# W1's loads of the merged stage: a pause while block 2's tokens are turned, then even distances

## The chip, the cores and the metric

The kernel runs on one core of one Trainium2 chip. A time is the device time of one execution in microseconds (us). Timed runs give a median; a separate profiled execution gives the trace, whose span (first to last instruction) is a little shorter than that execution's time.

## The reference

Three layers follow each other. All tensors are float32.

```python
# attention with random features: q, k, v are (4, 8, 576, 64)
q_p, k_p = phi(q_s), phi(k_s)            # exp(x @ omega.T - |x|^2/2 - max)
num = q_p @ (k_p.T @ v); den = q_p @ k_p.sum(0)
x = (num / den) as 2304 tokens of 512
# gated MLP, 512 -> 1536 -> 512
x = (sigmoid(x @ w_gate) * (x @ w_val)) @ w_out
# soft mixture of 8 experts with 4 slots each
logits = x @ phi                          # 2304 x 32
slots  = softmax(logits, over tokens).T @ x     # 32 x 512
slot_out[e] = relu(slots[e] @ w1[e]) @ w2[e]    # w1[e] 512 x 1024, w2[e] 1024 x 512
out = softmax(logits, over slots) @ slot_out
```

The change touches the loads of `w1` and four loads of `w2`. W1 is 16.8 MB, and the chip's on-core memory has no room for it while the MLP runs, so its pieces are loaded as buffers of the MLP come free.

## The kernel before, in words

The 2304 tokens are handled as five blocks: four of 512 (numbers 0 to 3) and one of 256 (number 4). Every float32 product of the MLP is three matmuls: each operand is split into a rounded high part and a remainder (`hi_of` on ScalarE, ACT, or VectorE, DVE; `lo_of` on GpSimd, POOL, or DVE). The MLP's weights lie in a DRAM buffer `wscr`, from where they are loaded again for each block or pair of blocks into `ws`.

The stages are, in order: attention and the first blocks (0 to 340 us), the pair of blocks 2 and 3 (to about 505 us), the merged stage (about 505 to 600 us), and the expert layers with the output.

**The merged stage** (`tail_jobs`, L1561) runs the last part of block 3, the products with `w_out` (`down_b`), together with the whole MLP of block 4 (`up_passes`, `down_c`). It has twelve steps, one for each 128 columns of the hidden layer. A step needs three weight pieces of 256 KB. `split_t` (L849) reads a piece from one of four slots of `ws`, splits it into a tile `w0`, `w1`, `w2` or `more`, and then `load_part` (L783) issues the load of a later piece into the same slot. These loads, `ws<-wscr`, are issued on SyncE's queue (SP). SP issues in order.

**Beside it** runs block 2's part in the expert layer (`m2_jobs`, L1650, with `moe2_chunks`, L1143): the logits, the turning of the block's tokens and the product into slots. The turning is four transposes on DVE (`chunk_x2`, L1108) and then sixteen moves of 64 KB between two buffers on the chip, `x2T<-x` (`chunk_back`, L1117), issued on SP too.

**W1's loads** (`load_w1`, L1163) are issued on ACT's queue, 512 KB each. The first eight (experts 0 and 1) have no floor, and the last two are issued late, when the slots are done. The other 22, and four loads of W2 into block 2's buffers (`free_x2`, L1198, on SP), take numbers 0 to 25 from one counter (`ring_of`, L1176) in the order in which the jobs are written: numbers 0 to 15 are experts 2 to 5, 16 is the first piece of expert 6, 17 and 18 two pieces of expert 7, 19 the next of expert 6, 20 to 23 the W2 loads, 24 and 25 the last of expert 6. A load with number k has the floor `BEGIN + PACE1 * k`, that is 478.0, 480.9, and so on to 550.5.

**What sets the order.** The kernel's text makes a list of operations with keys. A planner (`Plan.schedule`, L257) simulates them with a cost for each and hands out each engine's work in the order of the simulated times: an operation starts when its inputs and its buffer are ready, its engine is free and its floor (`plan.floor`) is past. Then the instructions are written down engine by engine in that order. A floor is a time of the plan, not of the chip: on the chip nothing waits for a clock. An engine issues its DMAs in the place that the plan gave them, each when its buffer is free. DMAs signal their end through eight counters, used in turn over both queues in the order of the plan, so a DMA is issued only when the one eight places before it has landed.

Of the kernel before, what the change touches and what calls it, by code (L numbers as in the profile page):

```python
# [81 lines left out]
M2 = 45.0  # L82
W1S = [1.0, 8.0, 15.0, 22.0, 24.0, 36.0, 50.0, 63.0, 29.0]
W2S = 2.0
BEGIN = 478.0
PACE1 = 2.9
TAIL0, TAIL1 = 2.75, 4.2
READY = 12.0
EARLY = 30
# [351 lines left out]
def body(ctx, tc, nc, qkT, tok, von, omT, wall, phi, w1, w2, ident_d, srep_d, rrep_d, mask_d, out):  # L441
    plan = Plan(nc)
# [713 lines left out]
    def pieces(tag, bufs=1, n=4):  # L1156
        if tag == "g1":
            halves = [half_region(k, F32) for k in range(2)]
            return [halves[c // 2][:, 1024 * (c % 2):1024 * (c % 2) + 1024] for c in range(n)]
        t = T([128, 1024 * n], tag, F32, bufs)  # L1160
        return [t[:, 1024 * c:1024 * c + 1024] for c in range(n)]

    def load_w1(x=None, cs=range(4)):  # L1163

        if x is None:
            e = len(W1)
            x = pieces(EXTAGS[e], 3 if EXTAGS[e] == "XT" else 1)
            W1.append(x)
        e = next(k for k, y in enumerate(W1) if y is x)
        for c in cs:  # L1170
            if 2 <= e < E - 1 or e == E - 1 and c > 1:
                plan.floor = BEGIN + PACE1 * ring_of("w1")
            ACT.dma_start(out=x[c], in_=w1[e, :, 1024 * c:1024 * c + 1024])
        plan.floor = 0.0

    def ring_of(name):  # L1176
        ring[name] = ring.get(name, -1) + 1
        return ring[name]

    def load_w2():  # L1180

        while len(W2) < len(ORDER2) and free:
            e, c = ORDER2[len(W2)]
            W2[e, c] = free.pop(0)
            SP.dma_start(out=W2[e, c], in_=w2[e, c])
# [12 lines left out]
    def free_x2():  # L1198

        for x in pieces("x2", 1, 2) + pieces("x2T", 1, 2):  # L1200
            free.append(x)
            plan.floor = BEGIN + PACE1 * ring_of("w1")
            load_w2()
        plan.floor = 0.0

# [42 lines left out]
    def last_slots():  # L1248
# [50 lines left out]
        si = T([128, 4, NSLOT], "si")  # L1299
        DVE.tensor_copy(out=si, in_=ps)  # L1300
        load_w1(W1[E - 1], (0, 1))
        plan.t = t0 + 7.0
        pr = bank("o3")[:, 0:NSLOT]
# [354 lines left out]
    for g, (j, f0, f1) in enumerate(GROUPS):  # L1658
        span = SPAN[g]
        if j == NB - 1:  # L1660
            m2_jobs(0, start + 3.0, 60.0)
            jobs += [(start + 4.0, "ex", load_w1), (start + 12.0, "ex", load_w1)]
            start = pair_jobs(start)
            jobs += [(start + W1S[k], "ex", load_w1) for k in range(4)]
            jobs += [(start + W1S[4 + c], "ex", lambda c=c: load_w1(W1[6], (c,))) for c in range(4)]
            jobs.append((start + W1S[4] - 0.01, "ex", big_regions))
            jobs.append((start + W1S[8], "ex", lambda: load_w1(W1[7], (2, 3))))
            jobs.append((start + M2 + W2S, "ex", free_x2))
            m2_jobs(PAIR[0], start + 1.0, M2)
            start = tail_jobs(start)  # L1670
            continue
        for f in range(f0, f1):
            jobs += moe_jobs(i, start + span * (f - f0) / (f1 - f0), span / (f1 - f0))
            i += 1
        units, a0, a1 = {0: (range(4, 8), LATE0 + 5 * LATE1, start + 0.92 * span),
                         1: (range(8, 16), start + LATE8 * span, start + span + SPAN[2] - READY - EARLY)}.get(g, ((), 0, 0))
        att = [c for u in units for c in step_chunks(u)]
        jobs += [(a0 + (a1 - a0) * k / len(att), "att", c) for k, c in enumerate(att)]
        if g == 2:
            m2_jobs(1, start + span / (f1 - f0), span * 0.7)  # L1680
        start += span
# [78 lines left out]
def build(nc, arrays):  # L1760
    args = [nc.dram_tensor(n, a.shape, mybir.dt.from_np(a.dtype), kind="ExternalInput").ap()
            for n, a in arrays.items()]
    args.append(nc.dram_tensor("out_0", (NTOK, DM), F32, kind="ExternalOutput").ap())
    with tile.TileContext(nc, schedule_with_timeline_sim=True) as tc:
        with ExitStack() as ctx:
            body(ctx, tc, nc, *args)
# [8 lines left out]
```

## Time and profile before

| | us |
|---|---|
| median of 3 runs (lowest, highest) | 665.77 (665.5, 667.17) |
| the profiled execution | 664.72 |
| its span | 662.6 |
| TensorE matmul (PE) busy | 640.8 (97%) |
| VectorE (DVE) busy | 482.3 (73%) |
| ScalarE (ACT) busy | 408.7 (62%) |
| GpSimd (POOL) busy | 266.4 (40%) |
| mean granted TensorE clock | 0.994 of full |

PE is busy nearly throughout, with float32 matmuls in three passes. The profile's page says that the DMA engines moved 134.27 MB, 203 GB/s in the mean, and shares out the chain of work that ended last as PE 85%, DVE 5%, DMA 4%. All engine work carries the line of one helper (L434), so rows are told apart by tile names: `ga`, `va`, `o` and `fl` are banks of accumulators, `w`, `more` split weights, `ws` the slots for weights, `g` and `XT` regions into which W1 is loaded, `x2T<-x` the turning moves.

### The profile page before, as it was taken

Reading aid. Unit: us, or ns where it says so; the run is one execution under the profiler, and the core shown is the slowest. Engines: PE = TensorE matmul, PEld = TensorE weight load, DVE = VectorE, ACT = ScalarE, POOL = GpSimd, SP = SyncE. Lnnn points to the kernel's source line nnn. Section 1 sums busy time; section 2 is a strip of 40 time slices with the busy share of each in tenths; the row PEclk is TensorE's granted clock in tenths of the full one; section 3 lists DMA queues with packets and bytes.
Section 4 is the critical chain, followed back from the end, with each engine's and each line's share of the span. In section 5 each row is a group of like instructions: output and inputs, shape, how many; then the busy total and the mean of one; then the engine's idle time right before and its main releaser. Section 6 shows DMA issues by size and latency. Waiting matters only on the chain.

```text
span 662.6 us, 12685 instructions
## 1 busy us (share of the span) xinstructions
PE 640.8 (97%) x4236; PEld 510.3 (77%) x4236; DVE 482.3 (73%) x1460; ACT 408.7 (62%) x937; POOL 266.4 (40%) x255
## 2 busy tenths in 40 slices
PE   7998999999999999999999999999999979999995
PEld 6675777778888788777877888788888878988663
DVE  5989998999899877788788966646647735545323
ACT  5999888889988867878775653443543412234012
POOL 1544444355544433336335455455553333321100
PEclk9999999999999999999999999999999989999998
DMA  7888666878886656533527732131226879736988
GB/s 251 314 274 265 240 216 207 259 234 275 277 279 222 208 152 231 187 96 112 160 80 240 224 108 62 36 95 36 79 77 223 242 247 313 269 106 226 405 337 242
DMA packets 61440, 134.27 MB, mean 203 GB/s; under 512 B 6848, under 2 KB 20928, under 8 KB 61376
## 3 DMA queue, kind: packets, MB, share of 16 engines
q1 hardware_dynamic: 55552, 116.11, 53.7%
q10 hardware_dynamic: 5824, 17.37, 8.0%
q8 instruction: 33, 0.54, 0.3%
q14 instruction: 31, 0.25, 0.1%
HBM read 113.00 MB, written 17.30 MB: 197 GB/s over the span
## 4 chain that ended last, share of the span: by engine, by line
PE 85%; DVE 5%; DMA 4%; issue 2%; SPq 1%; ACT 1%; POOL 1%; DVEq 0%; ACTq 0%; POOLq 0%
PE o L434 27%; PE fl L434 23%; PE va L434 18%; PE ga L434 17%; DVE g L434 2%; SPq L434 1%; DMA x2T<-x 1%; DMA ws<-wscr 1%; DMA g<-in_von 1%; DVE ga_a L434 1%; DMA g<-qscr 1%; DMA qscr<-g 1%; DVE g1b L434 0%; DVE x2T L434 0%; DVE x L434 0%
## 5 line engine op out<-in xcount | busy, mean ns | idle before, releaser
L434 POOL TENSOR_TENSOR w<-ws,w 128x512 fp32r<-128x512 f32 (+1 forms) x96 | 112.5, 1172 | 178.6 <-ACT w L434 46.8
L434 PE MATMUL o<-gt,w 128*128 128x512 f32 (+1 forms) x396 | 103.7, 396 | 0.0
L434 ACT ACTIVATE g<-g 128x128 f32<-128x128 f32 (+5 forms) x214 | 78.2, 422 | 15.5 <-DVE g L434 10.5
L434 PE MATMUL ga<-XT,w 128*128 128x512 f32 (+1 forms) x312 | 84.7, 400 | 2.3 <-POOL XT L434 1.3
L434 PE MATMUL fl<-g,g 64*128 64x128 f32 (+4 forms) x686 | 83.3, 313 | 3.6 <-DVE g L434 1.7
L434 PEld LDWEIGHTS o<-gt,w 128*128 128x128 f32 x396 | 71.7, 189 | 19.3 <-issue 3.3
L434 ACT ACTIVATE w<-ws 128x512 fp32r<-128x512 f32 (+1 forms) x87 | 49.4, 569 | 58.1 <-PE o L434 29.4
L434 PEld LDWEIGHTS fl<-g,g 64*128 64x128 f32 (+2 forms) x686 | 60.2, 182 | 24.2 <-issue 9.6
L434 PE MATMUL va<-XT,w 128*128 128x512 f32 x288 | 78.5, 403 | 0.0
L434 PEld LDWEIGHTS ga<-XT,w 128*128 128x128 f32 x312 | 54.9, 188 | 16.8 <-POOL XT L434 2.1
L434 PEld LDWEIGHTS va<-XT,w 128*128 128x128 f32 x288 | 52.5, 188 | 11.7 <-issue 1.3
L434 ACT ACTIVATE x2T<-g 128x512 f32<-128x512 f32 x72 | 46.0, 668 | 4.4 <-DVE x L434 3.5
L434 ACT ACTIVATE g1b<-g1b,g 128x128 f32<-128x128 f32 x128 | 40.5, 390 | 1.2 <-DVE g L434 1.2
L434 PE MATMUL o<-XT,w 128*128 128x256 f32 x264 | 36.8, 290 | 4.0 <-DVE ws L434 4.0
L434 PEld LDWEIGHTS o<-XT,w 128*128 128x128 f32 x264 | 35.2, 197 | 5.8 <-DVE ws L434 4.5
L434 DVE TENSOR_SCALAR x2T<-x2T 128x512 f32<-128x512 f32 (+1 forms) x72 | 36.3, 515 | 1.2 <-ACT x2T L434 1.0
L434 DVE CUSTOM_DVE_ANT_0 g<-fl,g 128x128 f32<-128x128 f32 x142 | 32.2, 284 | 3.1 <-PE fl L434 2.9
L434 POOL TENSOR_TENSOR g<-g 128x512 f32<-128x512 f32 (+1 forms) x20 | 23.0, 1149 | 28.5 <-DMA g<-in_tok 10.4
L434 ACT ACTIVATE ga_a<-ga_a 128x512 f32<-128x512 f32 x48 | 30.0, 624 | 3.2 <-DVE ga_a L434 2.9
L434 POOL TENSOR_TENSOR w<-x,w 128x512 fp32r<-128x512 f32 x17 | 21.8, 1285 | 23.6 <-ACT w L434 8.8
L434 DVE SCALAR_TENSOR_TENSOR x2T<-g,x2T 128x512 int32<-128x512 int32 x36 | 28.2, 785 | 0.1
L434 DVE TENSOR_REDUCE g<-g 128x8 f32<-128x512 f32 (+3 forms) x33 | 23.9, 726 | 5.9 <-POOL g L434 2.9
(310 smaller groups left out, 1361.7 us busy)
## 6 DMA issues: line engine op xcount, KB each, us to landing
ws<-wscr SPq DMA_DIRECT2D x37, 512.0 KB, 3.9
g<-in_wall SPq DMA_DIRECT2D x36, 512.0 KB, 5.0
ws<-wscr SPq DMA_DIRECT2D x52, 256.0 KB, 4.2
wscr<-x SPq DMA_DIRECT2D x36, 256.0 KB, 4.6
g<-in_qkT SPq DMA_DIRECT2D x15, 576.0 KB, 5.0
g<-in_tok SPq DMA_DIRECT2D x15, 576.0 KB, 5.2
g<-in_w ACTq DMA_DIRECT2D x16, 512.0 KB, 4.3
XT<-in_w ACTq DMA_DIRECT2D x12, 512.0 KB, 4.9
```

The lines of the kernel that those rows point to most:

```text
L434: ins = getattr(self.eng[e], method)(*a, **k)
```

## The change

The 26 numbered loads get other floors. Numbers 0 to 3 go to 476.0, 478.5, 481.0 and 483.5. Number 4 goes to 476 + 28 = 504.0 (it was 489.6), and from there each number follows the one before at 2.5 (it was 2.9), so that number 25 has 556.5 (it was 550.5). Nothing else is edited; the planner orders all operations anew with these floors.

```diff
-BEGIN = 478.0
-PACE1 = 2.9
+BEGIN = 476
+PACE1, FIRST1, GAP1 = 2.5, 4, 28.0
...
             if 2 <= e < E - 1 or e == E - 1 and c > 1:
-                plan.floor = BEGIN + PACE1 * ring_of("w1")
+                plan.floor = BEGIN + w1_at(ring_of("w1"))
             ACT.dma_start(out=x[c], in_=w1[e, :, 1024 * c:1024 * c + 1024])
         plan.floor = 0.0
+
+    def w1_at(k):
+        return PACE1 * k if k < FIRST1 else GAP1 + PACE1 * (k - FIRST1)
...
         for x in pieces("x2", 1, 2) + pieces("x2T", 1, 2):
             free.append(x)
-            plan.floor = BEGIN + PACE1 * ring_of("w1")
+            plan.floor = BEGIN + w1_at(ring_of("w1"))
             load_w2()
```

## Rows read from the trace of the kernel before

**Rows 1.** Windows: us; busy of PE, PEld, DVE, ACT, POOL; clock, DMA share, GB/s.

```profile
520.00:530.00 10.00, 9.92 (x67) 8.74 (x66) 7.93 (x22) 3.97 (x7) 2.87 (x2) 1.00 0.91 257
530.00:540.00 10.00, 5.98 (x39) 5.41 (x38) 3.61 (x7) 1.02 (x2) 2.56 (x2) 0.92 0.93 313
...
560.00:570.00 10.00, 10.00 (x72) 8.49 (x71) 6.34 (x12) 1.68 (x4) 3.24 (x3) 1.00 0.83 297
...
590.00:600.00 10.00, 10.00 (x93) 7.21 (x91) 4.58 (x17) 6.01 (x15) 2.22 (x3) 1.00 0.16 52
...
620.00:630.00 10.00, 10.00 (x177) 5.62 (x173) 3.48 (x13) 0.00 (x0) 0.00 (x0) 1.00 1.02 413
```

**Rows 2.** Timeline of PE (start, duration, operation; in brackets idle time and releaser).

```profile
525.69 0.30 PEld L434 LDWEIGHTS ga<-ga_a,more 128*128 128x128 f32 x2 [0.28 <-ACT more L434]
...
533.69 0.63 PE L434 MATMUL va<-gt,more 128*128 128x512 f32 x2
538.34 2.93 PE L434 MATMUL o<-XT,w 128*128 128x256 f32 x12 [4.02 <-DVE ws L434]
```

**Rows 3.** Windows cut at PE's stop.

```profile
534.40:538.34 3.94, 0.00 (x1) 0.00 (x1) 0.78 (x3) 0.00 (x0) 0.31 (x1) 1.00 1.02 378
538.34:541.80 3.46, 3.46 (x16) 3.46 (x17) 1.54 (x2) 0.36 (x1) 0.96 (x1) 0.51 0.51 179
```

**Rows 4.** Chain of waits, 513 to 539 us: start, duration, what.

```profile
517.77 6.77 DMA x2T<-x
...
524.55 0.34 ACTq L434
...
530.91 1.07 POOL w L434
531.98 5.45 DMA ws<-wscr
...
537.52 0.43 DVE w L434
537.95 0.34 DVE ws L434
```

**Rows 5.** Timeline of ACT and POOL: the split `more`.

```profile
525.01 0.63 ACT L434 ACTIVATE more<-ws 128x512 fp32r<-128x512 f32 x1 [0.97 <-POOL w L434]
525.72 1.57 POOL L434 TENSOR_TENSOR more<-ws,more 128x512 fp32r<-128x512 f32 x1 [0.85 <-ACT more L434]
```

**Rows 6.** Timeline of SP's queue: the first and last moves, one between, the next load.

```profile
514.48 0.52 SPq L434 DMA_DIRECT2D x2T<-x  x1
...
524.20 0.51 SPq L434 DMA_DIRECT2D x2T<-x  x1
...
529.52 0.51 SPq L434 DMA_DIRECT2D x2T<-x  x1
530.12 0.53 SPq L434 DMA_DIRECT2D ws<-wscr  x1
```

**Rows 7.** Waits of SP's queue, 513 to 531 us: total, times, longest.

```profile
SPq L434 <- DMA g<-in_w: 3.5, 2, 2.8
```

**Rows 8.** DMA issues: KB, median us to landing; 513 to 530, then 300 to 500 us.

```profile
x2T<-x SPq DMA_DIRECT2D x16, 64.0 KB, 4.9
...
x2T<-x SPq DMA_DIRECT2D x32, 64.0 KB, 2.5
```

**Rows 9.** Timeline of ACT's queue: W1 issues with numbers 0, 11, 16 and 25.

```profile
498.79 0.33 ACTq L434 DMA_DIRECT2D g<-in_w  x1
...
531.75 0.34 ACTq L434 DMA_DIRECT2D g<-in_w  x1
...
551.75 0.33 ACTq L434 DMA_DIRECT2D g<-in_w  x1
...
578.28 0.34 ACTq L434 DMA_DIRECT2D g<-in_w  x1
```

**Rows 10.** Loads into `ws`, 548 to 590 us: issue to landing.

```profile
DMA to landing us min/median/max: 2.5/4.2/5.3
```

## The prediction

> **What bounds the kernel now.** I read the windows of ten microseconds first. TensorE (PE) is busy through nearly every one of them; the reader is to see the one that is not, 530 to 540 us, where PE has 5.98 of 10 us and the DMA engines a share of 0.93 [rows 1]. So time is to be had only where PE stops, and around the change it stops once. The timeline of PE shows the stop: the last matmuls before it end at 533.69 + 0.63 = 534.32, and the next twelve start at 538.34 after 4.02 us, released by VectorE (DVE) writing `ws` [rows 2]. Cut at that point, the windows show a second cost: over 538.34 to 541.80 the granted clock is 0.51, that is 1.2 in place of 2.4 GHz, while it is 1.00 in the idle piece before and 0.92 over the whole ten [rows 1, 3]. In those 3.46 us PE does what takes about half of that at full clock, so 3.46 / 2 = 1.73 us are lost. The stop costs 4.02 + 1.73 = 5.75 us.
>
> Why it stops I read from the chain of waits, backwards. PE waited for the DVE write of `ws` at 537.95, which stood in DVE's queue behind the cast `w` at 537.52, and that cast waited for a load of weights, `ws<-wscr`, issued at 531.98 and 5.45 us under way [rows 4]. The chain puts the issue at 531.98 down to GpSimd's (POOL's) `w`. I don't follow it there. The five weight slots are given back in the order of their splits, and the slot of this load was given back by the split before that one, `more` at 525.72 + 1.57 = 527.29 [rows 5]. The load was late because its queue was: SyncE (SP) issues in order, and before this load it had to issue sixteen moves `x2T<-x`, the turning of block 2's tokens, from 514.48 to 529.52, and one weight load at 530.12 [rows 6]. In program order the DMAs take eight completion counters in turn, over both queues, and each waits for the one eight places before it. That is why a move, which touches nothing that W1 touches, was issued only at 524.20: SP had stood for a W1 load, 2.8 us at the longest and 3.5 us in two waits [rows 6, 7]. The same tie runs the other way. The W1 issue on ScalarE's (ACT's) queue at 524.55 waited for a move that was 6.77 us under way [rows 4], and the split `more` queued behind it, with ACT idle for 0.97 us, then kept PE's weight load waiting for 0.28 us [rows 5, 2].
>
> The moves themselves are slow in this stretch: 4.9 us in the median from issue to landing, where the thirty-two moves of blocks 0 and 1, with only W1's eight loads without floor in that stretch, took 2.5 us [rows 8].
>
> **The change part by part.** No transfer is added or removed: 26 floored transfers (22 of W1, and 4 of W2 which share the counter) keep their sizes and queues, and only their earliest planned times move.
>
> First, when they run. A floor is a planned time, and the trace runs behind it by a shift that the W1 issues themselves show: 498.79 for floor 478.0 (number 0) is 20.8; 531.75 for 509.9 (number 11) is 21.9; 551.75 for 524.4 (number 16) is 27.4; 578.28 for 550.5 (number 25) is 27.8 [rows 9]. The step from 21.9 to 27.4 is the stop again, 5.5 us of shift that PE does not make up later. With the new floors and 21.7 us of shift, numbers 0 to 3 (476 to 483.5) run at about 497 to 505 us, and number 4 (504) at about 525.7. Between 505 and 525.7 no W1 load is issued, where there are seven now (numbers 3 to 9). The moves, which start at 514.48, lie in the pause.
>
> Then SP. Sixteen moves and two weight loads follow each other at the 0.6 us that a move's issue takes, 18 x 0.63 = 11.3 us, if no counter holds them up. A counter comes round after eight issues, 5 us; a landing of 2.5 us, as in blocks 0 and 1, is well inside, and even 4.9 us just is. So SP is through with the moves at about 525.8 in place of 530.0. ACT has no W1 issue to stand at: `more` starts about 0.8 us earlier, and its POOL half ends near 526.4. The late load is then issued at 526.4 instead of 531.98.
>
> What it needs: PE ran out of work at 534.32, and from landing (537.43) to PE's restart (538.34) passed 0.91 us, so a landing by 533.4 costs PE nothing. At 5.45 us, as now, it lands at 531.9; at 4.2 us, the median of the later weight loads with W1 beside them [rows 10], at 530.6. Even the slowest of 548 to 590 us, 5.3 us, leaves over a microsecond. I take 5.45, the row nearest in place. The slowest move of the turning, a smaller transfer, took 6.77 us; taken for the weight load it gives 533.2, still in time by 0.2 us. So the stop goes: 4.02 + 1.73 + the 0.28 of ACT's hold-up = 6.03 us. At the upper end the 0.97 us of ACT's idle time come back whole, 6.7 us; at the lower, a landing a microsecond later than any here leaves a short stop, 5 us.
>
> What is late next: the even train after the pause. It has 22 transfers in 504 to 556.5, 52.5 us, where they had 60.9 us. 524 KB per 2.5 us is 210 GB/s in place of 181; three weight loads of 262 KB per step of 7.05 us add 112. That is 321 GB/s against 292. The window 560 to 570 moved 297 GB/s at a share of 0.83 with PE busy for all of it, so 321 would be a share of 0.90; the same engines moved 413 GB/s at 620 to 630 [rows 1]. I price the faster train at nothing. Its cover is the time between a weight load's issue and its split, in which landings of up to 5.3 us cost PE no wait [rows 10]; without that cover each of seven further steps would pay. Below nothing it can't be: with fewer loads in flight no row here shows PE faster.
>
> The Trainium skill (DMA: Bandwidth & Descriptors, section "Where 436 GB/s comes from") says that HBM binds a core at some 358 GB/s. By it, 321 GB/s would have 37 GB/s left and the crowding rival below would be near; its time of 663 us would be mine. The trace disagrees: 413 GB/s out of HBM in [rows 1]. I go by the trace.
>
> Two smaller edits cost nothing. The first four loads come about 2 us earlier, beside PE work that needs few transfers. The last one, floor 556.5, runs at 556.5 + 22 = 578.5 where it ran at 578.28, and is followed by a stretch whose DMA share is 0.16 (590 to 600) [rows 1]. With the merged stage ending 6 us sooner it still lands before the expert layers, which come after 605.
>
> The sum is made against the profiled execution: 664.72 - 6.03 = 658.7 us. The runs shown have their median 1.05 us above it, 665.77, so the time that a median would show is 659.7 us.
>
> **The rivals.**
> *The resumed train crowds the weights once.* The weight loads of 525 to 534 us share the engines with four W1 loads instead of the moves. For it: at a share of 0.93 the late load needed 5.45 us, and landings spread. Against: the moves, which made the share high at only 257 GB/s (520 to 530), are done by then. If a stop of 1.5 us remains and the clock falls after it as it does now, the gain is 6.03 - 1.5 - 1.73 = 2.8 us: 663 us.
>
> *The W1 loads were not the cause.* The moves have short rows and one slow issuer; if they alone make SP late, the stop stays and the time is 665.8 us. Against: blocks 0 and 1, and SP's waits for W1 by name [rows 8, 7]. The case in which the pause lies beside the moves in time, so that the change does not do what it says, has the same price; it needs a shift wrong by 8 us or more, where the issues agree within 1.1 us before the stop.
>
> *Slower.* The place is the seven steps from 542 to 590 us. Each weight load there has so far landed in 5.3 us or less. If the train drives the engines to their limit, landings grow as they did around 524 to 532 us, to some 7 us, and every step waits 7 - 5.3 = 1.7 us: 7 x 1.7 = 11.9, with the clock falling at least once, 13.6, less 6.0 of gain: 7.6 us slower, 673 us. It decides from the point at which 321 GB/s can't be moved at a share under 1. Against it stands 413 GB/s in [rows 1].
>
> **How the numbers follow.** Forecast 0.74, one crowded stop 0.11, no gain 0.07, slower 0.08. A change of 0.3% is 2.0 us, about what a measurement of this kernel can tell from none. Faster by more: 0.74 + 0.11 = 0.85; within: 0.07; slower: 0.08. The forecast's own range is 658.5 to 661 us (6.7 to 5 us of gain, with the spread of the medians). Widened to take in the crowded stop, it is 658 to 664 us; the other two cases, with 0.15, and a little of the rest stay outside.
>
> **What would show it.** Right: no PE wait over 1 us between 525 and 600 us, granted clock 1.00 there, SP's list of waits without W1 loads up to 526, moves landing in about 2.5 us, last move issued before 526.5, and the whole chain after 540 shifted by 5.5 to 6.5 us. Wrong: a PE wait on `ws` again near 534, or new waits of DVE or ACT on `ws<-wscr` every 7 us after 540.

## The result, and the profile after

| | before | changed |
|---|---|---|
| median of 7 runs each, us | 667.17 | 662.54 |
| lowest and highest | 665.5, 668.73 | 660.38, 663.57 |
| ratio, 95% interval | | 0.9917 (0.9894 to 0.9940) |
| profiled execution, span | 664.72, 662.6 | 660.38, 658.6 |

The change made the kernel faster by 4.6 us in the medians; 6.0 had been forecast. The ratio's interval, taken of 667.17 us, is 4.0 to 7.1 us, so it holds both numbers. In a second comparison on the chip (run e10 below) the ratio was 0.9927 (0.9901 to 0.9953).

The windows of the changed kernel, with the columns of [rows 1]:

```profile
510.00:520.00 10.00, 10.00 (x84) 8.52 (x83) 6.91 (x13) 5.72 (x9) 2.77 (x3) 1.00 0.33 87
520.00:530.00 10.00, 10.00 (x71) 9.27 (x70) 6.59 (x16) 6.26 (x9) 3.89 (x3) 1.00 0.62 167
530.00:540.00 10.00, 9.15 (x64) 8.17 (x64) 7.17 (x13) 2.63 (x4) 4.98 (x4) 1.00 0.96 345
...
560.00:570.00 10.00, 10.00 (x68) 9.20 (x67) 4.27 (x8) 1.63 (x4) 3.88 (x3) 1.00 0.88 295
...
590.00:600.00 10.00, 10.00 (x91) 8.66 (x88) 6.82 (x28) 5.42 (x16) 2.59 (x2) 1.00 0.27 68
```

The reader sees the pause (a DMA share of 0.33 at 510 to 520, where it was 0.76), the resumed train (0.96 at 530 to 540) and what is left of the stop: PE is busy for 9.15 of those ten microseconds, where it was 5.98, and the clock is 1.00, where it was 0.92 [rows 1].

PE's one stop in the stage, in its timeline, and the wait of SP's queue on W1 in 513 to 531 us (total, times, longest), which answers to [rows 7]:

```profile
536.59 0.61 PE L434 MATMUL o<-XT,w 128*128 128x256 f32 x3 [0.85 <-DVE ws L434]
```
```profile
SPq L434 <- DMA g<-in_w: 1.8, 1, 1.8
```

That wait lies behind the late weight load in SP's queue: it ended at 530.29, when the W1 load issued at 525.82 had landed. No move and neither of the first two weight loads behind the moves stood for W1.

The DMA issues of 513 to 530 us (count, KB, median us to landing), against [rows 8]: the moves are twice as fast. Of the weight loads, the two in the pause are faster too (2.9 and 3.8 us, where their like took 5.3 and 4.9); the three issued from 527.00 on, beside the resumed W1 loads, take 6.2 to 6.5 us.

```profile
ws<-wscr SPq DMA_DIRECT2D x5, 256.0 KB, 6.2
x2T<-x SPq DMA_DIRECT2D x16, 64.0 KB, 2.6
```

The chain of waits that ended in this stop (start, duration, what), against [rows 4]:

```profile
527.42 0.20 DVE ws L434
527.63 6.38 DMA ws<-wscr
534.00 0.03 issue
...
534.13 0.43 DVE w L434
534.56 0.20 DVE cT L434
534.75 1.45 DVE ga_a L434
536.20 0.34 DVE ws L434
536.54 0.04 issue
```

The late weight load is issued at 527.63 instead of 531.98, but takes 6.38 us instead of 5.45, and between its landing and PE's restart lie two more operations of DVE, `cT` and `ga_a`.

**A measure with less noise.** The runs of one kernel spread over several microseconds, and most of that arises before the change has any effect: over the twelve profiles of the table the merged stage begins anywhere from 501.0 to 505.8 us. So I compare profiles by the time from the first of PE's twelve `o<-gt,w` (502.74 us before, 503.81 changed) to the end of the span: "the stage" from here on. Each kernel has one profile. The two of the changed kernel (changed and e10) differ by 0.65 us, as much as their stops do (0.85 and 1.51), so a difference of a few tenths between two kernels is not told by this measure.

```
kernel                     ratio (95%)             stage us  PE stop us  clock after it  moves land
before                     1                       159.90    4.02        0.51            4.9
changed                    0.9917 (0.9894-0.9940)  154.78    0.85        1.00            2.6
e10 changed, again         0.9927 (0.9901-0.9953)  155.43    1.51        1.00            2.3
e1  pause, old distance    0.9947 (0.9920-0.9973)  157.70    2.08        0.64            2.9
e2  distance, no pause     0.9953 (0.9927-0.9979)  158.71    3.07        0.58            4.6
e4  new order, old loads   0.9975 (0.9947-1.0002)  158.76    3.12        0.56            4.7
e3  old order, new loads   0.9898 (0.9869-0.9927)  154.30    none                        2.4
e8  old order, pause only  0.9892 (0.9857-0.9927)  154.44    none                        2.2
e9  old order, pace only   1.0013 (0.9985-1.0041)  161.74    3.74, 0.76  0.50            5.6
e7  old order, own counter 0.9900 (0.9863-0.9937)  155.21    0.82        1.00            4.9
e5  old order, few bytes   0.9928 (0.9904-0.9952)  155.42    1.19        1.00            2.4
e11 new order, later       0.9896 (0.9865-0.9926)  153.56    none                        2.1
```

Ratio: runs of the kernel against runs of before on the same chip; all other columns come from one profile each. "Moves land" is the median in the window from 510 or 513 to 530 us (532 in e2, 534 in e9, to take in all sixteen).

### The profile page after: what moved, and what is told of

The parts are those of the page before. It is cut to its first block, busy times and chain, and to the rows that moved or that the text cites. A ratio compares the mean times of both kernels' runs of the same rounds, so it can differ in the third digit from the quotient of the medians.

```text
span 658.6 us, 12689 instructions
## 1 busy us (share of the span) xinstructions
PE 639.2 (97%) x4236; PEld 508.8 (77%) x4236; DVE 484.6 (74%) x1460; ACT 410.5 (62%) x937; POOL 269.1 (41%) x257
## 4 chain that ended last, share of the span: by engine, by line
PE 76%; DMA 8%; DVE 7%; ACT 3%; issue 3%; SPq 1%; POOL 1%; DVEq 0%; POOLq 0%; ACTq 0%
PE o L434 24%; PE fl L434 20%; PE va L434 16%; PE ga L434 16%; DVE g L434 3%; DMA qscr<-g 2%; DMA g<-in_tok 2%; DMA ws<-wscr 2%; SPq L434 1%; DMA g<-qscr 1%; DMA g<-in_wall 1%; DVE ga_a L434 1%; ACT ga_a L434 1%; ACT g L434 1%; DVE g1b L434 1%
```

## The experiments

My theory: with the pause the moves, and the weight loads behind them on SP, are free of W1's loads, and that is the whole gain. The rivals: the closer distance makes it; or the planner, which got other floors, wrote another order for all engines, and that order makes it. The orders do differ: e3's expectation counts 168 of PE's matmuls and 56 of DVE's instructions in other places than before (the traces, which leave out buffer numbers, show 93 and 56), and some splits changed their engine.

**e1: the pause alone, at the old distance.**

```diff
-BEGIN = 476
-PACE1, FIRST1, GAP1 = 2.5, 4, 28.0
+BEGIN = 478.0
+PACE1, FIRST1, GAP1 = 2.9, 4, 26.0
```

> The old start and distance (478.0, 2.9) with the pause alone: number 4 at 504.0, the last at 564.9. Theory (the pause frees the moves, and the weight load behind them, from W1's loads): PE's stop near 536 us is under 1.5 us, the clock stays at 1.00, ratio to before 0.990 to 0.994. Rival (the closer distance makes the gain): the stop of some 4 us stays, ratio 0.998 to 1.002. The distance of 2.9 crowds the resumed loads less, so by the theory the stop is no longer than the 0.85 us of the changed kernel.

The moves were freed (2.9 us), but a stop of 2.08 us stayed and the time missed the theory's range. **e2: the distance alone.**

```diff
-PACE1, FIRST1, GAP1 = 2.5, 4, 28.0
+PACE1, FIRST1, GAP1 = 2.5, 26, 0.0
```

> The new start and distance (476, 2.5) without the pause: number 25 at 538.5, so that nine loads in place of seven fall between 505 and 525 us. Theory of the pause: the moves land in 4.9 us or more again, a stop of 4 us or longer stays near 536 us with the clock falling after it, ratio 0.999 to 1.006. Rival (the distance makes the gain): ratio 0.990 to 0.994.

The moves were slow and a stop of 3.07 us stayed, in kind as the theory expected, though shorter than its 4 us; yet the runs were faster than before by 0.5%, which was not expected. Both misses have one cause, as e8 and e9 below show: each set of floors gets another order from the planner, so neither run changed one thing. The next two hold the order.

**e3: the order of before, only the loads moved.** After the planner has run with the old floors, loads 4 to 25 alone are put elsewhere in its list; every instruction of PE, DVE, POOL and ACT other than the loads stays in its place.

```diff
-        for _, i, (e, method, a, k) in self.schedule():
+        order = list(self.schedule())
...
+        order.sort(key=lambda x: place_of(*x))   # load k >= 4: at TO(k), once its buffer is free
+        for _, i, (e, method, a, k) in order:
...
+def TO(k):
+    return 504.0 + 2.5 * (k - 4)
```

> The order of before for every engine's work, with only the numbered loads 4 to 25 moved to the places of the new floors (504 and then every 2.5); numbers 0 to 3 stay. Theory (transfers): the stop goes to under 1 us as the profile of before foretold it, ratio 0.989 to 0.993. Rival (the planner, given other floors, put 168 of PE's matmuls and 56 of DVE's operations in other places, and that made the gain): the stop stays at 3 to 4 us, ratio 0.998 to 1.002.

**e4: the order of the changed kernel, the loads put back** in the same way, with `TO(k) = 478.0 + 2.9 * k`.

> The order of the changed kernel for every engine's work, with the numbered loads 4 to 25 moved back to the places of the old floors (478.0 + 2.9 k). Theory (transfers): the moves land in about 5 us again and a stop of 3 us or more comes back, ratio to before 0.998 to 1.003. Rival (the planner's order): the stop stays under 1.5 us, ratio 0.990 to 0.994.

Together they answer. Moving the loads alone takes 5.60 us off the stage and leaves PE no stop at all. The new order alone takes off 1.14 us and leaves a stop of 3.12 us; its ratio, just under the theory's 0.998, can't be told from 1. The windows of e3 from 520 us on, where [rows 1] has 5.98:

```profile
520.00:530.00 10.00, 10.00 (x73) 9.18 (x72) 7.76 (x20) 3.21 (x6) 3.64 (x3) 1.00 0.69 213
530.00:540.00 10.00, 10.00 (x72) 9.12 (x72) 6.44 (x12) 2.35 (x5) 4.10 (x4) 1.00 0.96 339
540.00:550.00 10.00, 10.00 (x69) 9.21 (x69) 5.04 (x9) 2.91 (x5) 3.88 (x3) 1.00 0.98 348
```

PE never stops, although the share is 0.96 and more. With the loads at these places, the order that the planner wrote for the changed kernel therefore cost 0.5 to 1.1 us of stage (154.78 and 155.43 against 154.30). The ratios of runs don't settle this small difference; their intervals overlap.

**e8 and e9: pause and distance apart, in the old order.** As e3, with `TO(k) = 504.0 + 2.9 * (k - 4)` and `TO(k) = 476.0 + 2.5 * k`.

> The order of before for all work, loads 4 to 25 moved to 504 and then every 2.9 (the last at 564.9): the pause at the old distance, without the planner's new order. Theory (the pause frees the moves; the planner's order spoiled part of it with the pause at the old distance): no stop over 0.5 us, stage from the first twelve o<-gt,w to the end 154.0 to 154.8 us, ratio 0.988 to 0.992. Rival (the distance of 2.5 is needed for the gain): the stop of 2 us stays as with the pause alone in the planner's order, stage 157 us or more, ratio 0.994 to 0.997.

> The order of before for all work, loads 4 to 25 at 476 + 2.5 k (486 to 538.5): the new distance without the pause and without the planner's new order. Theory of the pause: moves land in 4.5 us or more, a stop of 4 us or longer near 538 us with the clock falling, stage 159.5 to 162 us, ratio 0.999 to 1.006. Rival (the distance makes the gain): stage under 156 us, ratio 0.989 to 0.993.

Both came as the theory said, but for e9's stop: 3.74 us, and an earlier one of 0.76, where one of 4 us or longer was expected. The pause takes off 5.46 us by itself, and the distance adds nothing to it that these profiles can tell (154.44 against 154.30). Without the pause the closer distance costs 1.84 us of stage in the one profile; the interval of its ratio has 1 in it. In e9 PE's stop and the clock behind it (windows with the columns of [rows 3]), and SP's waits for W1, are the picture of before, only worse:

```profile
541.41 2.93 PE L457 MATMUL o<-XT,w 128*128 128x256 f32 x12 [3.74 <-DVE ws L457]
```
```profile
541.41:545.00 3.59, 3.59 (x17) 3.59 (x17) 1.54 (x2) 0.48 (x1) 0.97 (x1) 0.50 1.01 383
```
```profile
SPq L457 <- DMA g<-in_w: 5.0, 4, 2.3
```

**e7: the bytes stay, the counters go.** What of W1's loads does the harm: their bytes in flight, or the eight counters which they share with SP's DMAs? Loads 4 to 9 go to another queue, which has counters of its own.

```diff
+            if 489.0 < self.floors[i] < 505.0:
+                e = "POOL"
             for e, method, a, k in [p[0] for p in k["parts"]] if method == "together" else [(e, method, a, k)]:
                 ins = getattr(self.eng[e], method)(*a, **k)
```

In the kernel the line that unpacks follows with the changed engine.

> The kernel before with the loads 4 to 9 issued on GpSimd's queue in place of ScalarE's, at the same planned times. Their transfers then run beside the moves as before, but take completion counters of their own, so that neither SP nor ScalarE can stand at a counter for them. If the counters carry the harm, SP's waits name no W1 load, the last move is issued before 527 us and PE's stop near 538 us falls under 1.5 us; ratio to before 0.990 to 0.995. If the bytes in flight carry it, the moves still land in 4.5 us or more, SP stands at the counters of its own moves, and a stop of 2.5 us or more stays; ratio 0.997 to 1.005. GpSimd's own time for issuing may add up to 6 us of its queue, which would show as later splits on GpSimd.

Its DMA issues of 510 to 530 us and SP's waits on DMAs:

```profile
g<-in_w POOLq DMA_DIRECT2D x5, 512.0 KB, 4.9
ws<-wscr SPq DMA_DIRECT2D x4, 256.0 KB, 4.8
x2T<-x SPq DMA_DIRECT2D x16, 64.0 KB, 4.9
```
```profile
SPq L436 <- DMA x2T<-x: 1.6, 2, 1.4
SPq L436 <- DMA ws<-wscr: 0.6, 1, 0.6
```

The moves are as slow as before (4.9 us), and still most of the gain is there: no wait of SP for W1, sixteen moves issued in 11.6 us (517.51 to 529.06) instead of 15.0, and the old stop gone. PE's one stop, 0.82 us, is another: it ends 2.6 us later in the stage (543.95 - 505.75 = 38.2 us from its start, against 35.6), and the load behind it, issued at 535.80 and 7.2 us under way, is the third after the one that was late before. The six issues took GpSimd 3.5 us in all. The last move came after the 527 us that I had named, but this stage began 3.0 us later than that of before. So the harm went mainly by the queues being tied to each other. The run takes two ties at once, SP's to W1's counters and ACT's to the moves'; it doesn't part them.

**e5: the counters stay, the bytes go.** As e3, but loads 4 to 9 keep their old places with 32 of 1024 columns, and the rest follows at the new places.

```diff
+        late = [(place_of(*x), x[1], (*x[2][:3], {n: y[:, 32:1024] for n, y in x[2][3].items()}))
+                for x in order if 489.0 < self.floors[x[1]] < 505.0]
...
+        order = [(t, i, (*alt[:3], {n: y[:, 0:32] for n, y in alt[3].items()}) if 489.0 < self.floors[i] < 505.0 else alt)
+                 for t, i, alt in order]
```

> The order of before for all work. The loads 4 to 9 stay at their old places on ScalarE's queue with their counters, but load only the first 32 of each 1024 columns (16 KB in place of 512); the other 992 columns, and the loads from 10 on, come at the places of the new floors. It completes a square: before has bytes and counters beside the moves, GpSimd's queue had bytes alone, the pause in the old order has neither, and this one has counters with next to no bytes. A counter is held only as long as its transfer is under way, so if the harm is the bytes' slow landing passed on by the counters, the small loads land in some 2 us and do no harm: moves land in 2 to 3 us, no stop over 0.5 us, stage 154.2 to 155 us, ratio 0.988 to 0.992. If the number of DMAs on the eight counters is itself the harm, SP's waits come back, the last move comes 13 us or more after the first, a stop of 1 us or more stays, stage over 155.5 us.

Neither theory was right. The moves land in 2.4 us, and the first fifteen are issued at their own pace, 516.28 to 526.20. Then SP stands for W1 twice:

```profile
SPq L461 <- DMA g<-in_w: 2.7, 2, 1.4
```

The first wait is for a small load: the last move (528.75) stood for one which ACT had issued only at 525.53. The chain of waits shows what the second one did:

```profile
525.99 0.63 ACT more L461
526.62 0.02 issue
526.64 0.84 ACT L461
527.48 3.68 DMA g<-in_w
531.16 0.02 issue
...
531.23 4.92 DMA ws<-wscr
536.15 0.03 issue
...
536.24 0.43 DVE w L461
536.67 0.34 DVE ws L461
```

A weight load of SP (531.23) stood for a W1 load that ACT had issued only at 527.48, after its own work. A shared counter ties SP to when ACT gets to its DMA as well as to how long the DMA takes. But that W1 load is not one of the small ones. The DMA issues of 527.3 to 527.6 us give its size:

```profile
g<-in_w ACTq DMA_DIRECT2D x1, 496.0 KB, 3.7
```

It is the first of the 992-column rests, resumed after the pause; with six more DMAs in the program it stands eight places before the weight load. So the stop of 1.19 us came from a resumed large load on a shared counter. The small loads cost SP the first wait, and what they would cost PE by themselves this run doesn't show.

**e11: the order of the changed kernel, resumed 4 us later**, as e4 with `TO(k) = 508.0 + 2.5 * (k - 4)`.

> The order of the changed kernel for all work, with the numbered loads from 4 on moved from 504 to 508 and then every 2.5 (the last at 560.5). Theory (the 0.85 us that were left are the resumed loads crowding the weight loads issued at 527 to 528 us): the late weight load lands in under 5 us in place of 6.4, the stop near 536 us is under 0.3 us, stage 153.9 to 154.6 us, ratio 0.988 to 0.992. Rival (the stop comes from the planner's order of the splits and of DVE's work alone): the stop of 0.8 to 1.5 us stays, stage 154.7 to 155.5 us.

The stop is gone, the weight loads of 526 to 540 us land in 4.8 us in the median (6.3 in the changed kernel), and the stage is the shortest of all, 153.56 us, under the theory's range and 0.74 us under e3. So the planner's order need not be the slower one where no stop is left. Its windows:

```profile
520.00:530.00 10.00, 10.00 (x66) 9.05 (x65) 6.27 (x16) 7.43 (x10) 4.15 (x4) 1.00 0.54 136
530.00:540.00 10.00, 10.00 (x74) 9.36 (x74) 7.68 (x14) 2.59 (x4) 5.52 (x5) 1.00 0.91 309
```

What was left of the changed kernel's stop thus needed two things: W1 loads resumed (525.82 and 527.47) beside the weight loads, and the planner's order. Take away either, as e11 and e3 do, and it is gone.

**e10: the changed kernel once more**, beside the runs of e7, e8 and e9.

> The changed kernel once more, beside the same runs of before as the three others. Ratio 0.990 to 0.994 as the first time; stop of 0.8 to 0.9 us near 536 us. If the order that the planner wrote costs what the moved loads alone suggest, it stays some 0.1 to 0.3% slower than the pause in the old order.

The stop was 1.51 us this time, more than the 0.8 to 0.9 expected; the late load took 6.79 us. By ratio e3, e8, e11 (0.989 to 0.990) stand ahead of the changed kernel (0.992 and 0.993); they beat both kernels in the median, with intervals that still touch those of the change.

## Why the prediction was right, and where it was off

The measured 662.54 us lies in the stated range, but in the part that was added for a crowded stop; the forecast's own range ended at 661. Of the 2.8 us above the forecast's 659.7, half is the kernel before, which ran at 667.17 us in this comparison and at 665.77 when the sum was made; the other half is gain that did not come.

**What bounds the kernel and why PE stops: right, with one wait left out.** One stop, caused by a weight load late on SP behind moves that stood for W1's counters; e7 shows the tie, e3 and e8 the gain without it. The profile's own label for the issue at 531.98, POOL's `w` [rows 4], could rightly be left aside: that split ran to 530.91 + 1.29 = 532.20, past the issue.

```profile
530.91 1.29 POOL L434 TENSOR_TENSOR w<-ws,w 128x512 fp32r<-128x512 f32 x1 [3.61 <-DVE w L434]
```

What the load stood for last, from 530.65 to 531.93, was a move: the one issued at 526.01 and 5.9 us under way, which held the counter eight places before. The waits of SP's queue before, in 513 to 535 us:

```profile
SPq L434 <- DMA g<-in_w: 3.5, 2, 2.8
SPq L434 <- DMA x2T<-x: 2.3, 2, 1.3
```

So the slow moves held up SP too, 2.3 us beside the 3.5 us for W1 by name, and the prediction's "even 4.9 us just is" inside a round of the counters did not hold. The slots of `ws` in turn are five, as the prediction has it; the front of this text says four.

**When the loads run: right.** Number 4 was forecast at 525.7 us and was issued at 525.82; the pause held all moves but the last, which was issued at 526.32 (525.8 forecast, 529.52 before). They landed in 2.6 us (2.5 forecast). The train after it moved 317 GB/s at a share of 0.92 over 530 to 580 us (321 at 0.90 forecast).

**The sum: 6.03 forecast, 5.12 measured in the stage.** By terms:
- the clock after the stop, 1.73: gained whole;
- ACT's hold-up at 525.69, 0.28 [rows 2]: gone;
- the stop, 4.02: 3.17 gained, 0.85 left (1.51 in e10). This is the step that failed.

It failed in the sentence "a landing by 533.4 costs PE nothing". Relative to the start of the stage that is 30.66 us; the load landed at 534.00 - 503.81 = 30.19, in time by the forecast's own measure. But the forecast took over the 0.91 us from landing to restart from the order of before, and the planner wrote another: from 534.00 to 536.59 it took 2.59 us, as DVE had `cT` and `ga_a` between the cast and the write of `ws`. The `ga_a` cast took 1.53 us beside POOL's split; the same cast took 0.43 us alone in the trace of before. I had read the planner's order as fixed, though the front of this text says that it orders all anew. Where no stop is left, the gain in the stage is 5.46 to 6.34 us (e8, e3, e11), so the sum itself was sized about right.

Two of the signs that were named came out otherwise: e10 has a PE wait over 1 us, and the work behind the stop moved by 5.1 us in the stage (4.5 in e10) instead of 5.5 to 6.5.

**The landing of the late load:** 5.45 taken, 6.38 and 6.79 measured. The first rival, the resumed train crowding the weights once, was partly what happened; it was priced at 3.2 us and cost about one, since the clock did not fall.

**The faster train at nothing: right, with the pause.** e8 and e3 differ by 0.14 us. PE had no stop at shares of 0.96 to 0.98 and 339 to 348 GB/s (e3). So the slower rival was answered by e3 for the train after the pause, and its sign, at a much smaller size, showed in e9, where the close train met the moves. Its cover was larger than the 5.3 us that it was priced with: weight loads issued from 548 to 590 us took up to 5.7 us in the changed kernel and 6.8 us in e11, and PE did not stop.

**W1's loads as the cause:** the second rival fell with e3 and e8 on one side and e9 on the other.

## What to carry to other kernels

When DMAs of two queues share a few completion counters, a wait on a queue can be for a transfer that has nothing to do with it: look at how far apart the late DMA and its releaser stand in the program, and move the large transfers out of the stretch in which a chain of small ones must pass. Where a planner orders all work anew for each setting, hold its order and move only the thing in question: here that turned two unclear runs (e1, e2) into clear ones (e8, e9), and the pause in the old order gained at least as much as the change itself. And measure the stage from a landmark in the trace when the noise lies before it.

## What was not expected of the hardware

- The granted clock stayed at 1.00 after PE stops of 0.82 to 1.51 us (changed, e5, e7, e10), was 0.64 over 3.6 us after 2.08 us (e1), 0.56 to 0.58 over 3.5 us after 3.07 and 3.12 us (e2, e4), and 0.50 to 0.51 after 3.74 and 4.02 us. A stop cut short gives back more than its own length.
- A 64 KB move between two buffers on the chip landed in 2.1 to 2.9 us in the median with W1 paused and in 4.6 to 5.6 us beside it, at DMA shares under 1 (0.76 and 0.91 in the two windows of before from 510 to 530 us).
